# Decode attention with a token mixer on one core: the Mixer products of the eighth row move from ahead of the loop to behind it

## The chip, the core and the metric

The kernel runs on one core of a Trainium2 chip. Its engines are TensorE (PE in the profile), VectorE (DVE), ScalarE (ACT), GpSimd (POOL) and SyncE (SP, which here only asks for transfers). Each has its own queue and works through it in order; semaphores join the queues. The metric is the device time of one execution in microseconds (us), as a median of several runs. The profile is that of one execution.

## What is computed

There are 8 rows x (one new token each, 512 wide). Each is normalised; the normalised rows go through two blocks whose results are added to x.

```python
xn = _layernorm(x, axis=-1)
return x + _A_ref(xn, A_k_cache, A_v_cache, A_wq, A_wo) + _B_ref(xn, B_w1, B_b1, B_w2, B_b2)

# _A_ref: 8 rows, 32 query heads on 8 key heads, 8192 cached keys, head size 128
scores = jnp.einsum("bhqd,bhkd->bhqk", q, k) * (Dh ** -0.5)
p = _softmax(scores, axis=-1)
o = jnp.einsum("bhqk,bhkd->bhqd", p, v)
return o.reshape(B, Sq, Hq * Dh) @ wo

# _B_ref: token mixer with one token, F = 1792
h = _layernorm(x, axis=-1)                                  # (B, S, D)
u = jnp.einsum("bsd,sf->bdf", h, w1) + b1                  # (B, D, F)
u = _gelu(u)
y = jnp.einsum("bdf,fs->bds", u, w2) + b2                  # (B, D, S)
```

With one token the mixer of a row is, for each of its 512 channels, a sum over 1792 hidden units f of w2[f] x gelu(w1[f] x h + b1[f]). Keys and values are 268 MB each in float32, the query and output weights 8.4 MB each.

## The kernel before

**The attention.** Keys and values are handled in 32 pairs of key heads: 8 rows, 4 pairs (NG) each. One pair has 8.39 MB of keys and as much of values. A ring of five slots of 32 KB in each partition (`slots`, named raw) holds them; one pair's keys or values take two slots. Every transfer of keys and values is asked for on SP's queue (`load`, line 116), so in program order, and each waits there until the earlier readers of its slots are through. From pair 2 on, keys of even pairs lie in slots 1 and 2, of odd ones in 0 and 1, and values in 3 and 4 (pairs 0 and 1 and the last values are placed otherwise); of each pair the half in slot 1 is scored first (`score_half`, lines 384 to 389), so that the next keys can be asked for after it.

For a pair n: VectorE turns the keys in 32 x 32 blocks, in eight pieces (`turn`, line 275), and TensorE multiplies them with the placed queries (`scores`, line 284). `softmax_and_values` (lines 391 to 404) then puts in program order: the maximum (`top`), the first half of the values of pair n - 1 (`values`, line 322), the exponentials of pair n (`exps`: a product, three VectorE steps and the exp on ScalarE, line 304), the second half of the values of pair n - 1, the next transfer of values, and `send_on` (lines 307 to 311), which brings the exponentials into the places that the values need. `take` (line 329) copies the finished pair from PSUM on ScalarE, `total` and `place_at` bring a row's results into `OT`, which is multiplied with the output weights at the end.

Pairs 0 and 1 stand ahead of the loop, pairs 2 to 29 run in the loop (line 425, 7 rounds over 4 pairs each), and the last two, `LAST - 1` and `LAST` (30 and 31), behind it.

**The mixer.** One row's mixer is `mx_begin`, 14 steps `mx_step`, and `mx_end`:

- `mx_begin` (lines 354 to 356): VectorE copies a selector, TensorE spreads the row over all partitions into the PSUM tile `hb`.
- `mx_step(j)` (lines 358 to 363): ScalarE applies gelu for 128 hidden units into `g`, POOL multiplies with w2, and, but for j = 0, adds to the sum `acc` (named macc). There is one tile `g`, so a step's gelu waits for the add of the step before.
- `mx_end` (lines 365 to 370): TensorE adds up the partitions of the sum into the row that `bsel` picks, VectorE adds it to `yrow`.
- `warm` (line 373): one exp on a single column, which brings the exp table back onto ScalarE after gelu.

Each of the seven loop rounds does the steps of one row (5, 5, 4 and 0 of them behind its four pairs, `MIX`), and in its first pair ends the row of the round before: `mx_end(col * 2)`, then `mx_begin(col)`. The eighth row's begin and 14 steps are ahead of the loop, seven behind pair 0 and seven behind pair 1 (lines 412 to 423), and the first `mx_end` of the loop, at 0, adds it. Behind the loop `mx_end((B - 1) * B)` (line 454) adds the row of the last round.

**The end.** Behind the last pair's scores (lines 457 to 491) come the transfers of its values in two halves (slots 2 and 1) and of the output weights (`load_wo`, line 137: slot 0 in one piece, slot 3 in pieces of 8, 4, 2, 1 and 1 blocks). The tile `hb` then serves as `y`: four products with `spread` bring in `yrow` (line 470), both halves of the last values follow, `take`, `place_at`, 28 blocks of the output product into `sums` (line 477), their fold on ScalarE (line 479), the last four blocks and the fold into `y` (line 483), a copy (line 490) and the transfer out (line 491).

Of the kernel before, what the change touches and what calls it, by code (L numbers as in the profile page):

```python
# [8 lines left out]
F32 = mybir.dt.float32  # L9
# [5 lines left out]
B, D, HQ, HKV, SK, DH, F = 8, 512, 32, 8, 8192, 128, 1792  # L15
REP = HQ // HKV
P = 128
# [6 lines left out]
BS = W // B  # L24
NC = D // P
NF = F // P
# [3 lines left out]
LAST = N_PR - 1  # L30
# [8 lines left out]
ROUNDS = B - 1  # L39
WO_HIGH = (8, 4, 2, 1, 1)  # L40
MIX = (5, 5, 4, 0)
PAD = 96
QE = D // P
QN = HQ * DH
# [3 lines left out]
def attn_mixer_kernel(ctx: ExitStack, tc: tile.TileContext, x, kc, vc, wq, wo, w1, b1, w2, b2, out):  # L48
    nc = tc.nc
    place = ctx.enter_context(tc.tile_pool(name="place", bufs=1))  # L50
    pad = place.tile([P, PAD], F32, name="pad")

# [15 lines left out]
    ps_a = ctx.enter_context(tc.tile_pool(name="ps_a", bufs=4, space=PSUM))  # L68
# [4 lines left out]
    def misc():  # L73
        return ps_m.tile([P, 512], F32, name="misc")

    def big():
        return t2k.tile([P, 512], F32, name="t2k")
# [45 lines left out]
    def tile_at(a):  # L123
        return slots[:, a, :].rearrange("p (t d) -> p t d", d=DH)
# [91 lines left out]
    lr = const.tile([P, NG], F32, name="lr")  # L216
    rl = const.tile([P, 1], F32, name="rl")
    acc = const.tile([P, D], F32, name="macc")
    QZ = const.tile([P, B * NG, NB, REP], F32, name="qz")
    Z = const.tile([P, NG, NB, ZW], F32, name="z")  # L220
    nc.vector.memset(Z, 0.0)
# [35 lines left out]
    def q_place(g):  # L257
        m = misc()
        for q in range(NB):
            for s in range(2):  # L260
                nc.tensor.matmul(m[s * HP:(s + 1) * HP, q * B * REP:(q + 1) * B * REP], rep[:, q, :HP],
                                 QT[:, 2 * g + s].rearrange("p b r -> p (b r)"), start=True, stop=True)
        nc.scalar.copy(QZ.rearrange("p (b g) q r -> p g q b r", g=NG)[:, g],
                       m[:, :NB * B * REP].rearrange("p (q b r) -> p q b r", b=B, r=REP))

    def q_set(i, g, n):
        dst = Z[:, :, :, REP:].rearrange("p g q (a k r) -> p g q a k r", k=2, r=REP)
        for a in range(NB):
            x = slice(a * W, (a + 1) * W)
            src = QZ[x, i:i + n] if isinstance(i, int) else QZ[x, bass.ds(i, n)]  # L270
            nc.scalar.copy(dst[x, g:g + n, :, a, 0, :], src)
# [41 lines left out]
    def apart(d):  # L313
        tc.declare_no_dep(d.ins, group="landed", across_iterations=True, reason="waits on landed instead")

    def values(n, k, own=False):
        if not k:
            OD[n] = ps_a.tile([P, 512], F32, name="acc")
        v = tile_at(VAT.get(n, (3, 4))[k]).rearrange("p (c t) d -> p t c d", c=NCH)
        for t in range(CH_T):  # L320
            j = t % NB
            d = nc.tensor.matmul(OD[n][j * W:(j + 1) * W, :].rearrange("p (c d) -> p c d", c=NCH),  # L322
                                 PT[k][:, t * W:(t + 1) * W], v[:, t],
                                 start=(not k and t < NB), stop=(k == 1 and t >= CH_T - NB))
            if own:
                apart(d)

    def take(n):
        nc.scalar.copy(OB[:, n % NG, :], OD.pop(n))  # L329

    def total(lo, hi):
        x = slice(lo * W, hi * W)
        m = misc()
        for g in range(lo, hi):
            nc.tensor.matmul(m[g * W:(g + 1) * W, :1], ohg, lr[:, g:g + 1], start=True, stop=True)
        nc.vector.reciprocal(rl[x], m[x, :1])

    def place_at(lo, hi, col):
        x = slice(lo * W, hi * W)
        m = misc()  # L340
        for c in range(NCH):
            for g in range(lo, hi):
                nc.tensor.matmul(m[g * W:(g + 1) * W, :DH], pick[:, c, :], OB[:, g, c * DH:(c + 1) * DH],  # L343
                                 start=(c == 0), stop=(c == NCH - 1))
        t = big()[x, :DH]
        nc.vector.tensor_tensor(t, m[x, :DH], keep[x], op=ALU.mult)  # L346
        s4 = work.tile([P, W], F32, name="s4")[x]
        nc.vector.tensor_reduce(s4, t.rearrange("p (k c) -> p c k", k=NB), AX.X, ALU.add)
        to = OT[x, :, col:col + 1] if isinstance(col, int) else OT[x, :, bass.ds(col, 1)]
        nc.vector.tensor_tensor(to, s4.unsqueeze(2), rl[x].unsqueeze(2).to_broadcast([(hi - lo) * W, W, 1]), op=ALU.mult)  # L350
# [3 lines left out]
    def mx_begin(col):  # L354
        nc.vector.tensor_copy(hsel, spread[:, col:col + 1] if isinstance(col, int) else spread[:, bass.ds(col, 1)])  # L355
        nc.tensor.matmul(hb, hsel.to_broadcast([B, P]), hn, start=True, stop=True)  # L356

    def mx_step(j):
        g = one.tile([P, D], F32, name="g")
        nc.scalar.activation(g, hb, AF.Gelu_apprx_tanh, bias=b1t[:, j:j + 1], scale=w1t[:, j:j + 1])  # L360
        nc.gpsimd.tensor_tensor(g if j else acc, g, w2t[:, j:j + 1].to_broadcast([P, D]), op=ALU.mult)  # L361
        if j:
            nc.gpsimd.tensor_add(acc, acc, g)  # L363

    def mx_end(at):
        flat = bsel.rearrange("p a b -> p (a b)")
        nc.vector.tensor_copy(esel, flat[:, at:at + B] if isinstance(at, int) else flat[:, bass.ds(at, B)])  # L367
        m = misc()
        nc.tensor.matmul(m[:B, :], esel, acc, start=True, stop=True)  # L369
        nc.vector.tensor_add(yrow, m[:B, :], yrow)  # L370

    def warm():
        nc.scalar.activation(small.tile([P, 1], F32, name="warm"), nil, AF.Exp)  # L373
# [17 lines left out]
    def softmax_and_values(n, then, ready=None):  # L391
        mr = top(n)
        if ready is not None:
            nc.tensor.wait_ge(landed, 16)
            nc.tensor.sem_inc(landed, -16)
        if n:
            values(n - 1, 0, ready is not None)
        p = exps(n, mr)
        if n:
            values(n - 1, 1, ready is not None)  # L400
        d = then()
        if ready is not None:
            apart(d)
        send_on(p)
# [4 lines left out]
    score_half(1, True)  # L409
    load(kc, 2, home(2))  # L410
    softmax_and_values(0, lambda: None)
    mx_begin((B - 1) * BS)
    for j in range(NF // 2):
        mx_step(j)
    warm()

    score_half(1, False)
    softmax_and_values(1, lambda: load(vc, 1, 3))
    nc.tensor.sem_inc(landed, 16)
    take(0)  # L420
    for j in range(NF // 2, NF):
        mx_step(j)
    warm()

    with tc.For_i(FIRST, FIRST + ROUNDS * NG, NG, iteration_sync=SYNC) as i:
        col = i - FIRST
        j = 0
        for n in range(FIRST, FIRST + NG):
# [11 lines left out]
            if n == FIRST:  # L440
                mx_end(col * 2)
                mx_begin(col)
            for _ in range(MIX[n - FIRST]):
                mx_step(j)
# [7 lines left out]
    softmax_and_values(n, lambda: load(vc, n, 3), True)  # L452
    take(n - 1)
    mx_end((B - 1) * B)
    warm()

    n = LAST
# [6 lines left out]
    take(n - 1)  # L464
    total(0, NG)
    place_at(0, NG - 1, (B - 1) * BS)
    y = hb
    sums = ps_a.tile([P, D], F32, name="acc")
    for j in range(NB):
        nc.tensor.matmul(y[j * W:(j + 1) * W, :D // NB], spread, yrow[:, quarter[j]], start=True, stop=False)  # L470
    for k in range(2):
        values(LAST, k)
    take(LAST)
    place_at(NG - 1, NG, (B - 1) * BS)
    for c in range(FOLD):
# [43 lines left out]
```

## Time and profile before

| | us |
|---|---|
| median of 3 runs | 1301.0 (1300.29 to 1301.19) |
| the profiled execution, its own time | 1299.84 |
| its span | 1298.1 |
| TensorE busy | 732.7 (56%) |
| VectorE busy | 681.9 (53%) |
| POOL busy | 250.9 (19%) |
| ScalarE busy | 208.0 (16%) |
| gelus, line 360 (112) | 87.1, 0.778 each |
| multiplications on POOL, line 361 (112) | 116.4, 1.04 each |
| adds on POOL, line 363 (104) | 132.0, 1.27 each |
| read from HBM | 553.69 MB |

Busy times of engines overlap and are not to be added. In a row of the timeline stand the start, the busy time, the engine, the line, the operation, what it writes and reads with its shape, the number of instructions that were put together, and in brackets how long the engine had been idle and what ended that. PEld is TensorE's loading of weights. A "q" behind an engine's name is its queue (SPq, ACTq): instructions that the queue handles by itself, such as asking for a transfer. In a row of stretches stand the bounds, their length, the busy time and number of instructions of PE, PEld, DVE, ACT and POOL, the granted clock of TensorE as a share of full speed, the mean busy share of the 16 transfer engines, and GB/s.

### The profile page before, as it was taken

The numbers are of one execution on the slowest core, as the hardware profiler recorded it, in microseconds if no ns is written. First come the engines' busy times: TensorE is split into PE (matmuls) and PEld (weight loads), VectorE is DVE, ScalarE is ACT, GpSimd is POOL, SyncE is SP. The second block draws the span as 40 slices with busy tenths as digits, with TensorE's granted clock in tenths as the row PEclk, the third lists the DMA queues.
The fourth block names the chain that finished last, engine by engine and source line by source line (L and its number), as shares of the span: only waits on it lengthen the run. The fifth ranks groups of instructions, "written<-read, shape, count | busy, mean of one in ns | idle before, by whom it ended". The sixth has DMA issues, their size and how long they took to land. (4 is left out here: it accounts for less than half of the span.)

```text
span 1298.1 us, 12560 instructions
## 1 busy us (share of the span) xinstructions
PE 732.7 (56%) x4860; PEld 163.8 (13%) x4860; DVE 681.9 (53%) x557; ACT 208.0 (16%) x328; POOL 250.9 (19%) x225
## 2 busy tenths in 40 slices
PE   4372646546556655656655465654654664455766
PEld 1110111101111110111101111110111110111112
DVE  3665345565445665445656444656544556544560
ACT  0023221102220022201212012210222002220000
POOL 0036222103320033200332023220332003320000
PEclk9676788877778777788777878877788878778888
DMA  9996999999999999999999999999999999999998
GB/s 405 436 436 277 419 423 443 424 436 436 426 446 426 444 424 444 426 426 446 426 446 424 444 424 438 434 426 446 426 444 424 444 426 426 446 426 447 423 427 354
DMA packets 10978, 553.91 MB, mean 427 GB/s; under 512 B 1324, under 2 KB 1356, under 8 KB 1748
## 3 DMA queue, kind: packets, MB, share of 16 engines
q1 hardware_dynamic: 10836, 553.67, 98.6%
q8 instruction: 11, 0.18, 0.0%
q0 software_dynamic: 96, 0.02, 0.0%
q10 hardware_dynamic: 32, 0.02, 0.0%
q14 instruction: 3, 0.02, 0.0%
HBM read 553.69 MB, written 0.02 MB: 427 GB/s over the span
## 5 line engine op out<-in xcount | busy, mean ns | idle before, releaser
L275 DVE STREAM_TRANSPOSE raw<-raw 128x2048 f32<-128x2048 f32 x256 | 565.4, 2274 | 262.6 <-DMA raw<-in_A_k_cache_dram 253.1
L284 PE MATMUL acc<-raw,z 128*32 128x512 f32 x2048 | 367.4, 803 | 490.0 <-DVE raw L275 383.4
L322 PE MATMUL acc<-raw,pt 128*32 128x512 f32 x2048 | 240.1, 610 | 16.7 <-DMA raw<-in_A_v_cache_dram 12.9
L361 POOL TENSOR_TENSOR g<-g,pad 128x512 f32<-128x512 f32 x104 | 108.1, 1039 | 375.7 <-ACT g L360 375.7
L284 PEld LDWEIGHTS acc<-raw,z 128*32 128x32 f32 x2048 | 47.9, 123 | 789.3 <-DVE raw L275 517.7
L363 POOL TENSOR_TENSOR macc<-macc,g 128x512 f32<-128x512 f32 x104 | 132.0, 1269 | 8.2
L304 ACT ACTIVATE t2k<-acc,ns 128x512 f32<-128x512 f32 x32 | 22.0, 687 | 673.4 <-PE acc L322 603.4
L360 ACT ACTIVATE g<-hb,pad 128x512 f32<-128x512 f32 x112 | 87.1, 778 | 216.1 <-POOL macc L363 202.3
L311 DVE STREAM_TRANSPOSE pt<-misc 128x512 f32<-128x512 f32 x64 | 45.9, 717 | 133.3 <-PE misc L310 129.0
L361 POOL TENSOR_TENSOR macc<-g,pad 128x512 f32<-128x512 f32 x8 | 8.3, 1039 | 526.6 <-ACT g L360 526.6
L322 PEld LDWEIGHTS acc<-raw,pt 128*32 128x32 f32 x2048 | 65.0, 112 | 173.9 <-issue 150.7
L310 PE MATMUL misc<-t2k,send 128*128 128x512 f32 x128 | 66.9, 647 | 8.5 <-ACT t2k L304 8.5
L298 DVE TENSOR_TENSOR t2k<-misc,hmask 128x128 f32<-128x128 f32 x32 | 9.3, 292 | 113.8 <-PE misc L296 113.8
L291 DVE TENSOR_REDUCE mr<-acc 128x1 f32<-128x512 f32 x32 | 22.1, 690 | 54.9 <-PE acc L284 54.9
L360 ACT ACT_TABLE_LOAD x23 | 29.5, 1283 | 38.8 <-PE hb L356 38.6
L329 ACT COPY ob<-acc 128x512 f32<-128x512 f32 x32 | 18.7, 586 | 74.1 <-PE acc L322 74.1
L373 ACT ACT_TABLE_LOAD x23 | 29.5, 1283 | 0.4
L310 PEld LDWEIGHTS misc<-t2k,send 128*128 128x128 f32 x128 | 22.7, 197 | 51.2 <-issue 41.6
L242 PE MATMUL misc<-raw,ob 128*32 128x512 f32 x64 | 11.4, 880 | 11.3 <-DMA raw<-in_A_wq_dram 11.3
L356 PE MATMUL hb<-hn,hsel 8*128 8x512 f32 x16 | 9.9, 702 | 7.3 <-DVE hsel L355 7.3
L369 PE MATMUL misc<-macc,esel 128*8 128x512 f32 x16 | 8.1, 590 | 8.1 <-DVE esel L367 8.1
L346 DVE TENSOR_TENSOR t2k<-misc,keep 128x128 f32<-128x128 f32 (+2 forms) x9 | 2.6, 292 | 18.3 <-PE misc L343 18.3
(79 smaller groups left out, 135.3 us busy)
## 6 DMA issues: line engine op xcount, KB each, us to landing
raw<-in_A_v_cache_dram SPq DMA_DIRECT2D x4, 4096.0 KB, 36.4
raw<-in_A_wq_dram SPq DMA_DIRECT2D x2, 4096.0 KB, 17.0
raw<-in_A_k_cache_dram SPq DMA_DIRECT2D x2, 4096.0 KB, 30.8
raw<-in_A_wo_dram SPq DMA_DIRECT2D x1, 4096.0 KB, 29.4
raw<-in_A_wo_dram SPq DMA_DIRECT2D x1, 2048.0 KB
raw<-in_A_wo_dram SPq DMA_DIRECT2D x1, 1024.0 KB, 32.2
raw<-in_A_wo_dram SPq DMA_DIRECT2D x1, 512.0 KB
raw<-in_A_wo_dram SPq DMA_DIRECT2D x2, 256.0 KB, 33.2
```

Source lines behind the costliest of these rows:

```text
L275: nc.vector.transpose(t, t)
L284: nc.tensor.matmul(SD[n][c * W:(c + 1) * W, :].rearrange("p (t j) -> p t j", j=W), Z[:, n % NG, q, (1 - k) * REP:(1 - k) * REP + W], t[:, ...
L291: nc.vector.tensor_reduce(mr, SD[n], AX.X, ALU.max)
L304: nc.scalar.activation(p, SD.pop(n), AF.Exp, bias=ns, scale=SCALE, accum_out=lr[:, n % NG:n % NG + 1])
L310: nc.tensor.matmul(m, send[:, k, :], p, start=True, stop=True)
L311: nc.vector.transpose(PT[k][:, :CH_T * W], m)
L322: d = nc.tensor.matmul(OD[n][j * W:(j + 1) * W, :].rearrange("p (c d) -> p c d", c=NCH), PT[k][:, t * W:(t + 1) * W], v[:, t], start=(not ...
L329: nc.scalar.copy(OB[:, n % NG, :], OD.pop(n))
L360: nc.scalar.activation(g, hb, AF.Gelu_apprx_tanh, bias=b1t[:, j:j + 1], scale=w1t[:, j:j + 1])
L361: nc.gpsimd.tensor_tensor(g if j else acc, g, w2t[:, j:j + 1].to_broadcast([P, D]), op=ALU.mult)
L363: nc.gpsimd.tensor_add(acc, acc, g)
L373: nc.scalar.activation(small.tile([P, 1], F32, name="warm"), nil, AF.Exp)
```

## The change

The begin and the 14 steps of the eighth row leave the stretch ahead of the loop. `acc` is set to zero on POOL at its allocation, so that the loop's first `mx_end` adds nothing. Behind the loop, after the `mx_end` of the last round's row in the section of pair `LAST - 1`, come `mx_begin((B - 1) * BS)` and the first 11 steps (`LATE`); the other three follow in the section of `LAST`, behind `place_at`. The first half of the last pair's values is put ahead of `mx_end(0)`, which adds the eighth row to `yrow`; then come the four products with `spread`, and the second half of the values. The loop itself is not edited.

```diff
+LATE = 11
...
     acc = const.tile([P, D], F32, name="macc")
+    nc.gpsimd.memset(acc, 0.0)
...
     softmax_and_values(0, lambda: None)
-    mx_begin((B - 1) * BS)
-    for j in range(NF // 2):
-        mx_step(j)
     warm()
 
     score_half(1, False)
     softmax_and_values(1, lambda: load(vc, 1, 3))
     nc.tensor.sem_inc(landed, 16)
     take(0)
-    for j in range(NF // 2, NF):
-        mx_step(j)
     warm()
...
     take(n - 1)
     mx_end((B - 1) * B)
+    mx_begin((B - 1) * BS)
+    for j in range(LATE):
+        mx_step(j)
     warm()
...
     place_at(0, NG - 1, (B - 1) * BS)
+    for j in range(LATE, NF):
+        mx_step(j)
+    sums = ps_a.tile([P, D], F32, name="acc")
+    values(LAST, 0)
+    mx_end(0)
     y = hb
-    sums = ps_a.tile([P, D], F32, name="acc")
     for j in range(NB):
         nc.tensor.matmul(y[j * W:(j + 1) * W, :D // NB], spread, yrow[:, quarter[j]], start=True, stop=False)
-    for k in range(2):
-        values(LAST, k)
+    values(LAST, 1)
     take(LAST)
```

## The prediction

> **What bounds the kernel now.** I read the totals of the page first, then its transfer lines, then the stretches around the only slice in which the transfers fall off.
>
> ```profile
> span 1298.1 us, 12560 instructions
> GB/s 405 436 436 277 419 423 443 424 436 436 426 446 426 444 424 444 426 426 446 426 446 424 444 424 438 434 426 446 426 444 424 444 426 426 446 426 447 423 427 354
> ```
>
> No engine is busy for much over half of the span, while the transfers run at one rate in nearly every slice. The exceptions are the first slice (405), the last (354) and the fourth (277, from 97.4 to 129.8 us). By stretches (engines, granted clock, DMA share, GB/s):
>
> ```profile
> 110.00:118.50 8.50, 0.00 (x0) 0.00 (x0) 8.50 (x5) 1.56 (x2) 6.49 (x6) 0.57 0.93 401
> 118.50:130.80 12.30, 5.27 (x40) 1.66 (x44) 8.16 (x4) 3.82 (x5) 7.26 (x7) 0.61 0.00 1
> 130.80:140.00 9.20, 9.20 (x89) 2.75 (x85) 1.42 (x4) 0.78 (x2) 0.00 (x0) 1.00 1.04 420
> 200.00:1200.00 1000.00, 567.63 (x3738) 119.73 (x3730) 539.38 (x407) 162.38 (x254) 195.79 (x171) 0.80 1.00 434
> ```
>
> The reader is to see 434 GB/s over a thousand microseconds, and 1 GB/s for 12.30 us. So the kernel is bound by its transfers, but for one hole ahead of the loop's first transfer. The timeline says who makes the hole:
>
> ```profile
> 94.88 0.33 SPq L116 DMA_DIRECT2D raw<-in_A_v_cache_dram  x1
> ...
> 109.00 17.66 DVE L275 STREAM_TRANSPOSE raw<-raw 128x2048 f32<-128x2048 f32 x8 [0.42 <-issue]
> ...
> 125.41 0.78 ACT L360 ACTIVATE g<-hb,pad 128x512 f32<-128x512 f32 x1 [2.50 <-POOL macc L363]
> ...
> 125.53 8.36 PE L284 MATMUL acc<-raw,z 128*32 128x512 f32 x64 [17.71 <-ACTq L425]
> ...
> 130.82 0.35 SPq L116 DMA_DIRECT2D raw<-in_A_k_cache_dram  x1
> ```
>
> Pair 1's values are asked for at 94.88 and nothing follows until pair 3's keys at 130.82. Those need the slot that the first score half of pair 2 reads. VectorE has turned that half by 109.00 + 17.66/2 = 117.8, but TensorE stands 17.71 us until ScalarE's queue reaches the loop (line 425), and ScalarE is held by the fourteenth Mixer step (125.41), which waits for POOL. TensorE doesn't wait for POOL itself, whose queue comes later still (line 425, first and last start):
>
> ```profile
> L425 POOLq EVENT_SEMAPHORE  x1: 17/17/17, 127.3 to 127.3; - x1
> ```
>
> **What the removal is worth.** The hole in full-rate time: 12.30 us at nothing, 8.50 x (434 - 401)/434 = 0.65 ahead of it, 9.20 x (434 - 420)/434 = 0.30 behind: together **13.2 us**. All of it goes if pair 3's keys are asked for before pair 1's values have landed, near 118. The order without the steps:
>
> ```profile
> 95.00 3.64 PE L322 MATMUL acc<-raw,pt 128*32 128x512 f32 x32
> ...
> 95.76 0.15 DVE L302 TENSOR_SCALAR ns<-nb 128x1 f32<-128x1 f32 x1
> ...
> 101.02 0.78 ACT L360 ACTIVATE g<-hb,pad 128x512 f32<-128x512 f32 x1 [2.49 <-POOL macc L363]
> ...
> 103.00 1.26 POOL L363 TENSOR_TENSOR macc<-macc,g 128x512 f32<-128x512 f32 x1
> ...
> 103.22 0.67 ACT L304 ACTIVATE t2k<-acc,ns 128x512 f32<-128x512 f32 x1
> ...
> 104.04 3.78 PE L310 MATMUL misc<-t2k,send 128*128 128x512 f32 x4 [5.40 <-ACT t2k L304]
> ...
> 104.48 1.28 ACT L360 ACT_TABLE_LOAD   x1
> ...
> 1158.66 17.66 DVE L275 STREAM_TRANSPOSE raw<-raw 128x2048 f32<-128x2048 f32 x8 [7.72 <-DMA raw<-in_A_k_cache_dram]
> ...
> 1169.60 0.33 SPq L116 DMA_DIRECT2D raw<-in_A_k_cache_dram  x1
> ...
> 1262.88 1.98 PE L310 MATMUL misc<-t2k,send 128*128 128x512 f32 x4
> ...
> 1264.04 1.58 DVE L311 STREAM_TRANSPOSE pt<-misc 128x512 f32<-128x512 f32 x2 [3.75 <-PE misc L310]
> ```
>
> The median from issue to landing is on the page's last part:
>
> ```profile
> raw<-in_A_k_cache_dram SPq DMA_DIRECT2D x31, 28.4
> ```
>
> Pair 1's exp has its bias at 95.91, not 103.22. TensorE ends pair 0's second value half at 95.00 + 3.64 = 98.64 and sends on without having idled, so as at 1262.88: the transposes end 1264.04 + 1.58 - 1262.88 = 2.74 after its start, at 101.4; 0.42 for the loop's entry gives 101.8. Pair 2's keys are there: 118 less one transfer (two heads of 8192 x 128 x 4 bytes, 8.39 MB, at 434: 19.3 us) is 98.7. From VectorE's first turn to the next key transfer the loop takes 1169.60 - 1158.66 = 10.94, so the issue falls at **112.7**, some 5 us ahead of the landing. From then on each key issue has 28.4 - 19.3 = 9 us in hand, as in the loop now, so I expect no second hole.
>
> The other removals free nothing that ends last: hsel's copy and hb's product stand beside transfers. The added memset of the sum is on POOL, not over the 1.26 of an add of that size; POOL has nothing behind it until its first step, far on. The loop's first mx_end now adds zero, with the same instructions. SP's queue gets no new transfer.
>
> **What the end pays.** The eleven steps go behind pair 30's mx_end. How long that takes, from the loop, and the end as it stands:
>
> ```profile
> 144.09 1.02 PE L369 MATMUL misc<-macc,esel 128*8 128x512 f32 x2 [1.02 <-DVE esel L367]
> ...
> 145.14 0.68 DVE L370 TENSOR_TENSOR yrow<-misc,yrow 8x512 f32<-8x512 f32 x1 [1.20 <-PE misc L369]
> ...
> 148.52 0.78 ACT L360 ACTIVATE g<-hb,pad 128x512 f32<-128x512 f32 x1
> ...
> 153.71 0.78 ACT L360 ACTIVATE g<-hb,pad 128x512 f32<-128x512 f32 x1 [2.49 <-POOL macc L363]
> ...
> 1228.56 0.68 DVE L370 TENSOR_TENSOR yrow<-misc,yrow 8x512 f32<-8x512 f32 x1 [1.20 <-PE misc L369]
> ...
> 1260.40 0.69 ACT L304 ACTIVATE t2k<-acc,ns 128x512 f32<-128x512 f32 x1 [35.01 <-DVE ns L302]
> ...
> 1260.98 33.24 DMA raw<-in_A_wo_dram
> ...
> 1265.86 0.42 PE L470 MATMUL hb<-yrow,spread 8*32 8x128 f32 x8
> ```
>
> (The row of 1260.98 is from the chain of work that ended last.) I keep the clock of before; the hole shifts all alike. First gelu: 1228.56 + 3.38 = 1231.94. The third is 153.71 - 148.52 = 5.19 later, and each after it 2.49 + 0.78 = 3.27, so the eleventh stands at 1231.94 + 5.19 + 8 x 3.27 = 1263.3. ScalarE idles there now (35.01 us), but exp of pair 31 needs it at 1260.40. It now waits for the eleventh gelu and for warm's table: as exp came 2.20 behind the last gelu at 101.02, it comes at **1265.5, 5.1 late**. Queued behind it are TensorE's sending on (1266.4, as 104.04 is to 101.02; 3.5 late, and 3.78 long if the clock has fallen, so to 1270), VectorE's two transposes and pair 30's copy (to 1266.8). No transfer waits: the last weights are asked for at 1260.98 behind pair 30's values and land at 1294.
>
> Then three steps: 1.28 of table, gelus at 1268.1, 1271.4 and 1274.6, POOL done 103.00 + 1.26 - 101.02 = 3.24 after the last: **1277.9**. mx_end's product 1.02, yrow's sum 0.68, y's four products 0.42, handoffs: the last value half starts at **1280.2**. The first half (3.64) lies before and is hidden.
>
> ```profile
> 1274.90 5.34 PE L322 MATMUL acc<-raw,pt 128*32 128x512 f32 x32 [5.05 <-DMA raw<-in_A_v_cache_dram]
> ...
> 1280.29 0.59 ACT L329 COPY ob<-acc 128x512 f32<-128x512 f32 x1 [16.69 <-PE acc L322]
> ...
> 1282.83 0.21 DVE L350 TENSOR_TENSOR ot<-s,rl 32x32 f32<-32x32 f32 x1
> ...
> 1284.55 7.05 PE L477 MATMUL acc<-raw,ot 128*32 128x512 f32 x48 [2.56 <-DMA raw<-in_A_wo_dram]
> ...
> 1291.80 1.06 PE L477 MATMUL acc<-raw,ot 128*32 128x512 f32 x8 [0.19 <-DMA raw<-in_A_wo_dram]
> ...
> 1294.83 0.29 DVE L490 COPY g<-hb 128x128 f32<-128x128 f32 x1 [11.79 <-PE hb L483]
> ```
>
> Its row is 1274.90, so 5.3 late; but only 1.5 of slack (1283.04 to 1284.55) stood behind it. With the same 5.34 it ends at 1285.5, copy and placing 2.8, products at 1288.4. 56 of them at 3.64/32 us take 6.4, plus 1.7 of low clock (5.34 against 3.64): 8.1, to 1296.5; folding and the last products 1.9 (1291.80 + 1.06 to 1294.73): 1298.4, where it was 1294.73. **Loss 3.6.** Transfers no longer end last there, TensorE does.
>
> The low clock is the unknown. The value half alone at full clock: loss 1.9. Both pieces at full clock: 1280.2 + 3.6 + 2.8 + 6.4 + 1.9 = 1294.9, loss 0.2. Both at half throughout (7.3 and 12.7): loss 10.2. I take the row's own mixture, since the waits ahead are alike.
>
> On that the Trainium skill, "TensorE: Matmul & The Clock Gate", section "What's actually happening", has a rule: the clock drops to half after an idle window of about 3.4 us and returns after one busy window, both free-running. The row agrees (5.05 idle, then 1.70 lost). By that rule the new idle stretch, cut up by mx_end's product, might keep the clock, and the value half would then take 3.64; it might equally fall wrong.
>
> **Sum**: -13.2 + 3.6 = **-9.6**. The profiled execution took 1299.84 (span 1298.1 and 1.7 around it), which gives 1290.2; the median of the three runs is 1301.0, 1.16 higher, which would give 1291.4. I say 1291.0, nearer to the median, since medians are what is compared.
>
> **Rivals.**
> - *The end is hidden* (clock kept): -13.2 + 0.2 to 1.9, 1288 to 1290 beside the median and 1287 to 1288.5 beside the profiled execution. For it: TensorE gets work between 1278 and 1280. Against: 5.34 after a like wait. 0.15.
> - *The end is dear*: half clock through most of it, or further table loads (1.28 each) at pair 31's copy: loss 6 to 10, 1294 to 1298. For it: sending on at 104.04 took 3.78 instead of 1.98. Against: the last half of the values, after 5.05 of idling, lost only 1.70. 0.14.
> - *The wait at the loop's entry changes owner*: the change then doesn't do what it says. If another queue keeps TensorE from line 284, the key issue slides one for one from 118. From 118 + 13.2 - 3.6 = 127.6 on the hole costs as much as the end gains, and if it stays at 130.82 the kernel is **slower by 3.6**: 1304.6. For it: all queues pass line 425 and the trace names only the one that came last. Against: TensorE started 0.12 after ScalarE's step, and VectorE was in the loop by 109. 0.04 for slower, 0.04 for about even.
> - *A second hole*: an issue at 120 to 124 rather than 112.7 costs 2 to 6: 1293 to 1297. Margin 5 us. 0.05.
>
> **How the numbers follow.** My forecast's own span, 1289 to 1294, has 0.58. With the hidden end and the cheaper part of the dear one the range is 1287.2 to 1296.0. A measurement of this kernel can tell about 0.2%, 2.6 us: faster (under 1298.4) 0.92, same 0.04, slower 0.04.
>
> **What would show it.** The key issue behind 94.88 at 112 to 114 and TensorE's line 284 there waiting for VectorE; the fourth slice near 435 GB/s; pair 31's exp behind warm, not ns; yrow's last sum some 50 us behind pair 30's; line 322's last half released by it and not by a transfer. Wrong if the issue isn't ahead of the landing, if the first value half or the weights come late, or if the end takes over 7 us more.

## The result, and the profile after

| | before | changed |
|---|---|---|
| median of 6 runs, us | 1300.19 (1299.83 to 1301.19) | 1288.09 (1287.66 to 1289.92) |
| ratio of the times | | 0.9908, 95% interval 0.9895 to 0.992 |
| the profiled execution, us | 1299.84 | 1288.03 |
| its span, us | 1298.1 | 1286.2 |

The change makes the kernel faster by 12.1 us, or 0.9%; 9.6 were forecast. The first lines of the page after, and its chain of work that ended last:

```profile
span 1286.2 us, 12583 instructions
...
GB/s 409 426 439 441 432 433 431 436 436 426 442 432 430 442 428 434 442 428 434 440 428 436 436 432 436 426 440 436 426 442 432 430 442 428 434 442 427 437 423 329
...
PE 2%; POOL 2%; DVE 2%; ACT 1%; issue 0%; POOLq 0%; DVEq 0%
```

The fourth slice is now like the others (441, it was 277). The chain, which was 5% transfers and led back from the last weights, now holds engines only: at the end something else than a transfer is last. First the hole: the same stretches as in the prediction, of the changed kernel.

```profile
110.00:118.50 8.50, 4.26 (x32) 0.63 (x32) 8.50 (x5) 0.00 (x0) 0.00 (x0) 1.00 0.93 401
118.50:130.80 12.30, 10.44 (x77) 3.03 (x77) 3.14 (x7) 1.36 (x3) 0.00 (x0) 1.00 1.00 433
130.80:140.00 9.20, 2.76 (x4) 0.41 (x4) 1.05 (x4) 2.84 (x3) 1.93 (x2) 0.65 1.04 449
```

433 GB/s stand where 1 stood. The stretch ahead of it shows 401 in both kernels, so the 0.65 us that the prediction counted there was no part of the hole (without it the sum is 12.6). The timeline of the changed kernel at the loop's entry:

```profile
95.27 0.69 ACT L306 ACTIVATE t2k<-acc,ns 128x512 f32<-128x512 f32 x1 [19.03 <-DVE ns L304]
...
98.98 1.57 DVE L313 STREAM_TRANSPOSE pt<-misc 128x512 f32<-128x512 f32 x2 [3.83 <-PE misc L312]
...
101.38 17.66 DVE L277 STREAM_TRANSPOSE raw<-raw 128x2048 f32<-128x2048 f32 x8 [0.82 <-DMA raw<-in_A_k_cache_dram]
...
111.76 0.35 SPq L117 DMA_DIRECT2D raw<-in_A_k_cache_dram  x1
```

Pair 1's exp is on time, VectorE starts on pair 2's keys at 101.38 (forecast 101.8, and the keys had just landed), and pair 3's keys are asked for at 111.76 (forecast 112.7), well before pair 1's values land. Now the end (lines are two or three numbers higher than in the kernel before):

```profile
1242.69 5.34 PE L324 MATMUL acc<-raw,pt 128*32 128x512 f32 x32 [1.81 <-DMA raw<-in_A_v_cache_dram]
...
1249.04 0.15 DVE L304 TENSOR_SCALAR ns<-nb 128x1 f32<-128x1 f32 x1
1249.14 0.78 ACT L362 ACTIVATE g<-hb,pad 128x512 f32<-128x512 f32 x1 [2.51 <-POOL macc L365]
1249.93 1.28 ACT L375 ACT_TABLE_LOAD   x1
...
1251.34 0.67 ACT L306 ACTIVATE t2k<-acc,ns 128x512 f32<-128x512 f32 x1
...
1260.44 0.78 ACT L362 ACTIVATE g<-hb,pad 128x512 f32<-128x512 f32 x1 [2.49 <-POOL macc L365]
...
1263.72 1.88 PE L371 MATMUL misc<-macc,esel 128*8 128x512 f32 x2 [5.09 <-POOL macc L365]
1265.64 0.68 DVE L372 TENSOR_TENSOR yrow<-misc,yrow 8x512 f32<-8x512 f32 x1 [8.37 <-PE misc L371]
...
1267.04 5.13 PE L324 MATMUL acc<-raw,pt 128*32 128x512 f32 x32
...
1275.06 6.21 PE L480 MATMUL acc<-raw,ot 128*32 128x512 f32 x56 [1.10 <-DVE ot L352]
...
1283.00 0.29 DVE L493 COPY g<-hb 128x128 f32<-128x128 f32 x1 [8.00 <-PE hb L486]
```

The reader is to see the chain of the prediction link by link: the eleventh gelu (1249.14) stands ahead of exp, three gelus follow, POOL's last add releases the sum's product after 5.09 us of TensorE's idling, and the last value half starts behind yrow and not behind a transfer. The output products (line 480) don't wait for a weight any more: they wait for `ot`, and run through in 6.21 us. The granted clock of three of these rows, from the view of stretches (it stands third from the end):

```profile
1263.72:1265.60 1.88, 1.88 (x2) 0.10 (x2) 0.00 (x0) 0.00 (x0) 0.00 (x0) 0.50 1.01 436
1267.04:1272.17 5.13, 5.13 (x36) 1.15 (x32) 0.00 (x0) 0.00 (x0) 0.00 (x0) 0.70 0.99 425
1275.06:1281.27 6.21, 6.21 (x64) 2.02 (x68) 0.00 (x0) 0.00 (x0) 0.00 (x0) 1.00 0.68 274
```

The sum's product ran at half clock, the value half at 0.70, and the output products at full clock.

### The profile page after: what moved, and what is told of

Its sections match the earlier page's. It is cut to its first block, busy times and chain, and to the rows that moved or that the text cites. A ratio compares the mean times of both kernels' runs of the same rounds, so it can differ in the third digit from the quotient of the medians.

```text
span 1286.2 us, 12583 instructions
## 1 busy us (share of the span) xinstructions
PE 735.9 (57%) x4862; PEld 162.5 (13%) x4862; DVE 683.8 (53%) x559; ACT 206.5 (16%) x327; POOL 251.4 (20%) x226
## 5 line engine op out<-in xcount | busy, mean ns | idle before, releaser
L286 PE MATMUL acc<-raw,z 128*32 128x512 f32 x2048 | 371.3, 810 | 479.5 <-DVE raw L277 387.8
L324 PE MATMUL acc<-raw,pt 128*32 128x512 f32 x2048 | 243.8, 618 | 11.2 <-DMA raw<-in_A_v_cache_dram 7.8
L371 PE MATMUL misc<-macc,esel 128*8 128x512 f32 x18 | 10.0, 640 | 13.2 <-DVE esel L369 8.1
L372 DVE TENSOR_TENSOR yrow<-misc,yrow 8x512 f32<-8x512 f32 x9 | 6.1, 679 | 18.0 <-PE misc L371 18.0
```

The costliest lines, as they stand in the source:

```text
L286: nc.tensor.matmul(SD[n][c * W:(c + 1) * W, :].rearrange("p (t j) -> p t j", j=W), Z[:, n % NG, q, (1 - k) * REP:(1 - k) * REP + W], t[:, ...
```

## The experiments

Times are medians; the first four kernels share one set of runs of the kernel before (1300.57), the last four another (1300.85). Each ratio to it stands with its interval.

**The eighth row left out**

```diff
-    mx_begin((B - 1) * BS)
-    for j in range(LATE):
-        mx_step(j)
...
-    for j in range(LATE, NF):
-        mx_step(j)
...
-    mx_end(0)
```

> The eighth row's mixer is left out altogether, so the hole is gone and the end carries nothing for it. Theory (ScalarE's late queue makes the hole, transfers bind the rest, the moved sum costs a little at the end): the change's gain plus its loss at the end, 13.2 to 14.0 us under the kernel before, about 1286.4; the last product waits for the last weights again. If the move had cost nothing at the end: the same time as the changed kernel, 12.1 under. If the end's loss were 3.6 as forecast: 15.7 under.

Measured: 1287.24 (1287.17 to 1287.41), ratio 0.9899 (0.9884 to 0.9914), so 13.3 under before. The end of its chain of work, in order of time:

```profile
1249.70 31.92 DMA raw<-in_A_wo_dram
1281.62 0.04 issue
1281.66 0.47 PE hb L480 x8
```

The last weights end it again. What follows: the hole is worth 13.3 by the medians and 12.7 between the two profiled spans (1298.1 and 1285.4), near the 13.2 of the prediction; the sum without the 0.65 agrees with the spans. The moved row costs the changed kernel 0.9 by the medians and 0.8 between the spans, neither nothing nor 3.6. (The two medians are of different sets of runs; with each taken from its own before it is 1.2.)

**The eighth row at both places**

```diff
     softmax_and_values(0, lambda: None)
+    mx_begin((B - 1) * BS)
+    for j in range(NF // 2):
+        mx_step(j)
...
     take(0)
+    for j in range(NF // 2, NF):
+        mx_step(j)
```

> The eighth row is done ahead of the loop as before and once more behind it as in the change, so its mixer is added twice. The hole stays and the end's price is seen alone. By the prediction's sum 3.6 us slower than before (1303.8); by the changed kernel's trace, where transfers ended 13.9 earlier and TensorE 11.9, about 2.0 slower (1302.2). If transfers still ended last: within 0.5 of before.

Measured: 1303.68 (1302.14 to 1304.4), ratio 1.0023 (1.0013 to 1.0032), 3.1 over before. The timeline of its end:

```profile
1261.11 0.15 DVE L304 TENSOR_SCALAR ns<-nb 128x1 f32<-128x1 f32 x1
...
1266.42 0.67 ACT L306 ACTIVATE t2k<-acc,ns 128x512 f32<-128x512 f32 x1
...
1267.23 3.78 PE L312 MATMUL misc<-t2k,send 128*128 128x512 f32 x4 [3.31 <-ACT t2k L306]
...
1281.39 6.13 PE L324 MATMUL acc<-raw,pt 128*32 128x512 f32 x32
...
1290.39 6.21 PE L485 MATMUL acc<-raw,ot 128*32 128x512 f32 x56 [1.10 <-DVE ot L352]
```

The time lies between the two forecasts (3.6 and 2.0). The spans differ by 3.5, but 1.0 of that stands ahead of the end: in this profiled execution VectorE turned pair 30's keys at 1198.92, in that of the kernel before at 1197.96. So by the traces the end pays 2.5 with the hole in place, and 0.8 without it: the two parts don't simply add. The reason is below, in the point on the end. Exp is 1266.42 - 1261.26 = 5.16 behind its bias (forecast 5.1 late; an exp on time stands 0.1 behind its bias).

**Half of the steps ahead of the loop, behind pair 0**

```diff
     softmax_and_values(0, lambda: None)
+    mx_begin((B - 1) * BS)
+    for j in range(NF // 2):
+        mx_step(j)
     warm()
```

> Only the seven steps behind pair 0 stand ahead of the loop; the other half of the eighth row's mixer is left out, and nothing of it is behind the loop. Theory (the key issue slides one for one with what holds TensorE, and only what passes the landing of pair 1's values counts): pair 1's exp is late again, VectorE enters the loop at about 109, pair 3's keys are asked for near 120, about 2 behind the landing: 11 to 12 us under the kernel before (1288 to 1289). Rival (each step costs its share of the hole): half of the gain, 6.5 to 7 under.

Measured: 1288.44 (1288.15 to 1290.19), ratio 0.9913 (0.9898 to 0.9928), 12.1 under. Its timeline:

```profile
102.44 0.67 ACT L306 ACTIVATE t2k<-acc,ns 128x512 f32<-128x512 f32 x1
...
108.17 17.66 DVE L277 STREAM_TRANSPOSE raw<-raw 128x2048 f32<-128x2048 f32 x8 [0.42 <-issue]
...
118.55 0.36 SPq L117 DMA_DIRECT2D raw<-in_A_k_cache_dram  x1
```

Against the changed kernel, seven steps delay exp by 7.2 us (102.44 and 95.27) and the key issue by 6.8; the time is 1.2 over that of the kernel without the eighth row. Only what comes after the landing of pair 1's values costs time.

**The other half, behind pair 1**

```diff
     softmax_and_values(0, lambda: None)
+    mx_begin((B - 1) * BS)
     warm()
...
     take(0)
+    for j in range(NF // 2, NF):
+        mx_step(j)
     warm()
```

> Only the seven steps behind pair 1 stand ahead of the loop; the other half is left out, and nothing of it is behind the loop. Theory: exp is on time, but ScalarE's queue reaches the loop only with the last gelu, near 119.5, TensorE starts its four quarters there, pair 3's keys are asked for near 124.8, 6 us ahead of the kernel before: about 6 under (1294). Rival (ScalarE's queue isn't what holds TensorE; VectorE's start is): issue near 113 and 13 to 14 under.

Measured: 1295.6 (1293.74 to 1297.03), ratio 0.9961 (0.9948 to 0.9975), 5.0 under. Its timeline:

```profile
102.17 17.66 DVE L277 STREAM_TRANSPOSE raw<-raw 128x2048 f32<-128x2048 f32 x8 [0.42 <-issue]
...
120.70 0.78 ACT L362 ACTIVATE g<-hb,pad 128x512 f32<-128x512 f32 x1 [2.49 <-POOL macc L365]
120.82 9.52 PE L286 MATMUL acc<-raw,z 128*32 128x512 f32 x64 [19.83 <-ACTq L425]
...
127.28 0.36 SPq L117 DMA_DIRECT2D raw<-in_A_k_cache_dram  x1
```

Here VectorE enters the loop within 0.8 us of where it does in the changed kernel, and TensorE still stands 19.83 us, until 0.12 after the start of ScalarE's last gelu: ScalarE's queue holds it. The key issue is 3.5 earlier than before (127.28 against 130.82), and the profiled span is 3.6 shorter (1294.5 against 1298.1): one for one. The forecast of 6 was a little too good: from TensorE's start to the request it took 6.46 us here and 5.29 in the kernel before.

**POOL busy ahead of the loop, ScalarE free**

```diff
     take(0)
     warm()
+    h = one.tile([P, D], F32, name="g")
+    for _ in range(24):
+        nc.gpsimd.tensor_add(h, OB[:, 0, :], OB[:, 0, :])
```

> The changed kernel with 24 adds on POOL (some 30 us) into an unused tile ahead of the loop, behind pair 0's copy, with ScalarE left free: POOL's queue reaches the loop near 129. Theory (TensorE waits for ScalarE's queue, not for POOL's): no hole, the time of the changed kernel within 0.5 us. Rival (any late queue takes over the wait at the loop's entry): keys asked for near 134, a hole of 16 or more, 1303 or later.

Measured: 1289.01 (1288.52 to 1289.04), ratio 0.9909 (0.9892 to 0.9925). Its timeline, and from the view of line 425 when the two queues got there:

```profile
99.53 26.72 POOL L423 TENSOR_TENSOR g<-ob 128x512 f32<-128x512 f32 x24 [95.76 <-ACT ob L331]
...
104.41 1.80 PE L286 MATMUL acc<-raw,z 128*32 128x512 f32 x8 [3.70 <-issue]
...
112.27 0.35 SPq L117 DMA_DIRECT2D raw<-in_A_k_cache_dram  x1
...
1267.15 6.00 PE L324 MATMUL acc<-raw,pt 128*32 128x512 f32 x32
```

```profile
L425 ACTq EVENT_SEMAPHORE  x1: 17/17/17, 98.9 to 98.9; - x1
...
L425 POOLq EVENT_SEMAPHORE  x1: 17/17/17, 125.2 to 125.2; - x1
```

POOL comes 26 us after ScalarE, TensorE is in the loop long before, and there is no hole. A late queue as such doesn't hold TensorE; ScalarE's does. The time is 0.9 over the changed kernel, more than the 0.5 that the theory allowed, but the difference arises at the end: the last value half starts within 0.2 of where it did there (1267.15 against 1267.04) and takes 6.00 at a granted clock of 0.60, in place of 5.13 at 0.70.

**Eight steps and six in place of eleven and three**

```diff
-LATE = 11
+LATE = 8
```

> The changed kernel with 8 steps in pair 30's section and 6 in the last, instead of 11 and 3. Theory (the sum's chain ends last): pair 31's exp is on time, but the last pair's copy is behind the same values, so three gelus more follow it at 3.27 each: 9 to 10 us later than the changed kernel, about 1298. Rival (the delayed exp is what costs at the end): 2 us earlier than the changed kernel.

Measured: 1298.34 (1296.25 to 1298.97), ratio 0.9982 (0.9971 to 0.9992), 10.2 over the changed kernel. Each step behind the last exp costs a full 3.27 us, though exp itself is on time: the sum's product starts at 1273.51, 9.8 later than in the changed kernel, and the value half behind it takes 5.75 in place of 5.13. The sum's chain ends last, as the theory had it.

**Products in TensorE's idle stretch**

```diff
     values(LAST, 0)
+    m = misc()
+    for _ in range(5):
+        nc.tensor.matmul(m, ident, rep.rearrange("p q x -> p (q x)"), start=True, stop=True)
     mx_end(0)
```

> The changed kernel with five products of two constants into an unused tile between the first half of the last values and the wait for the mixer's sum, so that TensorE idles less there. Theory (2 us of the end are lost, nearly all of it to the low clock behind the idle 5.09 us): the sum's product takes 1.0 and not 1.88, the last value half 3.6 and not 5.1, and the end comes 1.5 to 2.2 us earlier, until the last weights bind: about 1286.2. Rival (the chain of sum, yrow and y is what costs, not the clock): the same time as the changed kernel, or later by what the products overrun.

Measured: 1287.2 (1287.1 to 1287.36), ratio 0.9896 (0.988 to 0.9913), 0.9 under the changed kernel. Its timeline:

```profile
1257.21 4.56 PE L473 MATMUL misc<-rep,ident 128*128 128x512 f32 x10
...
1262.40 1.02 PE L371 MATMUL misc<-macc,esel 128*8 128x512 f32 x2 [0.63 <-POOL macc L365]
...
1264.64 3.64 PE L324 MATMUL acc<-raw,pt 128*32 128x512 f32 x32
...
1271.86 8.27 PE L483 MATMUL acc<-raw,ot 128*32 128x512 f32 x56 [1.82 <-DMA raw<-in_A_wo_dram]
```

The sum's product takes 1.02 in place of 1.88 and the value half 3.64 in place of 5.13, as the theory said. But only 0.9 of these 2.4 is to be had, less than the 1.5 to 2.2 of the forecast, since then the last weights bind. The output products, now waiting for weights, take 8.27 at a granted clock of 0.79 and still end in time.

**All of the eighth row earlier behind the loop**

```diff
+    mx_end((B - 1) * B)
+    mx_begin((B - 1) * BS)
+    for j in range(9):
+        mx_step(j)
+    warm()
     n = LAST - 1
     score_half(n, True)
...
     take(n - 1)
-    mx_end((B - 1) * B)
+    for j in range(9, NF):
+        mx_step(j)
     warm()
...
     take(n - 1)
+    mx_end(0)
     total(0, NG)
```

> All of the eighth row's mixer behind the loop, but earlier: the last round's sum is taken right behind the loop, nine steps stand ahead of pair 30's scores in ScalarE's idle stretch of 36.9 us, five behind pair 30's values, and the sum ahead of the last placements. Theory: nothing of it ends last any more, the last weights bind the end, 2 us under the changed kernel, about 1286.2, and level with the kernel without the eighth row. Rival (steps beside the loop's exit or pair 30's scores delay exp or a transfer): later than the changed kernel.

Measured: 1287.27 (1287.16 to 1287.62), ratio 0.9897 (0.9881 to 0.9914): the time of the kernel without the eighth row, 0.8 under the changed one. The forecast gain of 2 was too high for the same reason: the last weights bind. Pair 30's exp came at 1216.21, 7 us later than in the changed kernel, and nothing waited for it that ends last. This version and the one with the products are the fastest measured here that do the whole work.

## Why the prediction was right, point by point

**The hole.** Forecast 13.2, measured 13.3 in medians and 12.7 in spans. Its cause is shown: with ScalarE late the wait is there (19.83 us), with only POOL late it isn't. Why the loop's entry makes TensorE wait for ScalarE's queue, no run shows. That the key issue counts from the landing of pair 1's values on is shown by the two halves: 12.1 and 5.0 under before, where a share for each step would have given the same for both. One term was wrong but small: the 0.65 ahead of the hole belongs to the stretch and not to the hole. A reading was off, too: pair 2's keys, put at 98.7, were there only just ahead of 101.38. It cost nothing, since VectorE's start was forecast for 101.8.

**No second hole.** Right: 433 and 449 GB/s up to 140 us, and no later slice of the page under 423 but the last.

**The late exp.** Forecast 5.1; behind its bias it came 5.16 with the row at both places, but 2.15 in the changed kernel (1249.19 to 1251.34), because there the first value half of pair 30 ran 5.34 us at a granted clock of 0.68 and the bias came later itself. That cost nothing.

**The sum's chain.** Forecast for the start of the last value half: 1280.2, less the 13.2 by which everything shifts, 1267.0. Measured 1267.04. That it is so near is luck, since two misses of about 1 us cancel. The eleventh gelu came at 1249.14, which is 14.2 earlier than the forecast 1263.3 and not 13.2. And the sum's product and y's four products took 1.88 and 0.65 at half clock, where 1.02 and 0.42 had been put.

**The price at the end** is the term that was mis-sized: 3.6 was forecast, 0.9 was measured (0.8 between the spans 1286.2 and 1285.4). That is why 12.1 were gained and not 9.6. Most of the difference is the low clock put on the output products: they were put at 8.1, with 1.7 of lower clock, and took 6.21; folding and the last products took 1.6 (1281.27 to 1282.84) and not 1.9. The rest is the end that they are measured against: without the row the last weights land only 12.6 earlier than in the kernel before (1281.62 and 1294.22), not 13.2.

Why does the same chain cost 2.5 with the hole? It starts at pair 30's keys, and these moved by more than the last weights. From the timelines of the kernel before and of the changed one:

```profile
1197.96 17.66 DVE L275 STREAM_TRANSPOSE raw<-raw 128x2048 f32<-128x2048 f32 x8 [9.08 <-PEq L515]
```

```profile
1184.07 17.66 DVE L277 STREAM_TRANSPOSE raw<-raw 128x2048 f32<-128x2048 f32 x8 [9.91 <-PEq L518]
```

The chain starts 13.9 earlier, the weights land 12.6 earlier. So without the hole the chain has some 1.3 us of room that the prediction didn't know of. The other 0.5 lies in the chain itself, which took 99.3 us from pair 30's keys to the last product with the row at both places and 98.8 in the changed kernel; its last value half took 6.13 there and 5.13 here. Most of the 1.3 can be seen in the last four us of the transfers, here of the kernel before (landing at 1294.22) and of the one without the eighth row (1281.62):

```profile
1290.22:1292.22 2.00, 1.81 (x20) 0.36 (x16) 0.00 (x0) 0.00 (x0) 0.00 (x0) 1.00 0.97 390
1292.22:1294.22 2.00, 1.82 (x40) 0.75 (x32) 0.00 (x0) 0.59 (x1) 0.00 (x0) 1.00 0.39 149
```

```profile
1277.62:1279.62 2.00, 1.85 (x20) 0.40 (x16) 0.00 (x0) 0.00 (x0) 0.00 (x0) 1.00 0.70 280
1279.62:1281.62 2.00, 1.81 (x40) 0.75 (x32) 0.00 (x0) 0.58 (x1) 0.00 (x0) 1.00 0.16 60
```

With the hole the transfers keep most of their rate until shortly before the last landing, without it they run out slowly; the missing 0.4 MB is 0.9 us at 434 GB/s. The kernel with the other half behind pair 1, whose hole is some 9 us long, ends like the kernel before (399 and 156), and the one with half of the steps behind pair 0, whose hole is some 1 us, lies between (326 and 86). Why a pause early on makes the end steeper wasn't found out, and no run here was made for it.

**The low clock** was rightly named as the unknown, and it fell both ways: the value half at 5.13 (forecast 5.34), the products at full clock. The same chain in the POOL kernel gave 6.00 for the value half, so the clock alone moves the end by 0.9. The rule cited there, the Trainium skill's "TensorE: Matmul & The Clock Gate", section "What's actually happening", has the clock fall after an idle window of about 3.4 us. One case here agrees: filling the 5.09 us of idling removed the lower clock from both products behind it. Another doesn't: in that same kernel TensorE idled for no more than 1.82 us at a time ahead of the output products, and they still ran at 0.79. When the clock falls was not settled here.

**The rivals.** No other queue took over the loop's entry, which the POOL kernel shows for the likeliest candidate. The second hole didn't come, and the end wasn't dear. By its size the result, 1288.09, lies just outside the forecast's own span (1289 to 1294) and where the first rival stood (the end hidden, loss 0.2 to 1.9, 1288 to 1290): the products did keep the clock, the value half did not.

## What to carry to other kernels

In a kernel that its transfers bind, look for the one stretch where they stop, and ask whose queue holds the next request: work with no tie to the request can hold it by standing ahead of a loop on an engine that another engine waits for at the entry. Work that is moved to the end is free only as far as the last transfer covers it, so put it as early behind the loop as its engine idles; here the last 0.8 us were to be had by that alone. A step's price isn't constant: seven steps cost 1.2 us or 8.4, by how far they held the request beyond the landing.

## What the runs showed of the hardware

While POOL adds, VectorE's small product of two SBUF tiles is held up. In the changed kernel:

```profile
1255.86 1.28 POOL L365 TENSOR_TENSOR macc<-macc,g 128x512 f32<-128x512 f32 x1
1255.99 1.22 DVE L352 TENSOR_TENSOR ot<-s,rl 96x32 f32<-96x32 f32 x1
```

The same instruction took 0.21 us in the kernel before (1266.71) and in the one without the eighth row (1255.43), where POOL had nothing to do. It ends just behind POOL's add. The Trainium skill, "SBUF — State Buffer", section "Who interferes with whom", says that a VectorE instruction with two inputs in SBUF blocks against a GpSimd instruction that reads SBUF, until the first is through; the row agrees. It cost nothing here, since VectorE's next wait is for the sum.
